# Seven products instead of eight: Strassen's scheme in the last MLP stage of an attention and MLP kernel

## The chip, the cores and the metric

The kernel runs on one core of a Trainium2 chip. The metric is the device time of one execution in microseconds (us). The engines are named as in the profile: PE (TensorE), DVE (VectorE), ACT (ScalarE), POOL (GpSimd) and SP (SyncE, which here only issues DMAs).

## The reference

```python
def attention(q, k, v, g_q, g_k):             # (8, 12, 448, 64) each, gains of 64
    q_n, k_n = rmsnorm(q, g_q), rmsnorm(k, g_k)
    scores = q_n @ k_n.T / 8
    attn = softmax(scores)                    # over the keys
    return attn @ v                           # f32

def mlp(x, w_in, w_out, alpha):               # x: 3584 x 768, w_in: 768 x 2048, w_out: 2048 x 768
    h = x @ w_in
    g = maximum(h, 0) + alpha * minimum(h, 0) # alpha: one slope for each of the 2048 columns
    return g @ w_out                          # f32

out = mlp(attention(...) as rows of tokens, w_in, w_out, alpha)
```

## The kernel before

The kernel works batch by batch (`B` = 8). The heads of a batch are taken in three groups of four heads (24 groups `y` in all). For each group q and k are loaded (tiles `nat`), squared on POOL (`sq`), summed on DVE, turned into a reciprocal root on ACT, and scaled (`qs`, line 179, on POOL for the later groups). A DMA on SP transposes them, and line 288 multiplies the transposed k by the gains on DVE. Then come the scores (`sc`), the exponentials (`expT`, ACT, line 343), the denominators and the products with v, whose result is `xT`.

For the third group of each later batch the denominator is prepared on POOL: `add_up` (line 356) adds the seven `expT` slices of the group into `rden` in six additions, and `den_pre` multiplies the sum by ones on PE (`dnb`, line 389). What follows `dnb` is a chain: two copies on DVE (line 397), a logarithm and an exponential on ACT (lines 401 and 410), a multiplication on DVE that writes `xT` (line 439).

The MLP runs one batch behind the attention. Its first product is cut into 16 units of 128 columns for each batch (`up`: six matmuls of 448 columns, ACT scales the result by alpha into `ah`, line 494, and DVE takes the maximum of both into `gT`, line 498). `gT` holds two batches side by side: 128 partitions by 16 column blocks (`NF`) by 896 tokens (`W`), the even batch in the first 448 tokens. Its second product is cut into units of one tile of 128 tokens and one half of the 768 outputs (`down`: 16 matmuls of 384 columns, a copy out of PSUM on DVE, line 520, and two stores of 64 rows, line 528). A pair of batches has 7 token tiles, and so 14 `down` units. The last unit of all is done in two halves of 192 columns with a store for each, half of its rows through ACT's queue.

The order on each engine is the order in which the Python code calls. A planner spreads the `up` and `down` units of a batch over the gaps between the attention steps of the next batch. Work that belongs to no gap is put behind a step with `after`. When the attention of the last batch is done, a list `rest` is left: the 16 `up` units of the last batch, one `down` unit left over from the even batch ahead of every third of them (`old`, five units: one of token tile 0, two each of tiles 1 and 2), and then the eight `down` units of tiles 3 to 6 (`new`):

```python
    ups, old, new = periods[B - 1]
    rest = []
    for n, u in enumerate(ups):
        if n % 3 == 0 and old:
            rest.append(old.pop(0)[1:])
        rest.append(u[1:])
    rest += [u[1:] for u in old + new]
```

PSUM has three pools: `pss` (tag `sc`, two tiles of two banks), `psa` (tag `acc`, one tile of two banks) and `psf` (tag `mm`, two banks). Units of `rest` take their bank from `psf`, every third from `psa`. In SBUF, `nat` has 6 buffers, `sq` 4, `qs` 4, `expT` `EB` = 3 and the result tiles `osb` 4.

Of the kernel before, what the change touches and what calls it, by code (L numbers as in the profile page):

```python
# [9 lines left out]
FP32 = mybir.dt.float32  # L10
FP16 = mybir.dt.float16
# [10 lines left out]
def kernel(  # L22
# [12 lines left out]
    nc = tc.nc  # L35

    B, H, S, D = q.shape
    DM = H * D
    DF = moe_w_in.shape[1]
    J = S // 64  # L40
# [3 lines left out]
    NF = DF // 128  # L44
    OH = DM // 2
# [4 lines left out]
    EB = 3  # L50
# [5 lines left out]
    ld = ctx.enter_context(tc.tile_pool(name="ld", bufs=2))  # L56
    att = ctx.enter_context(tc.tile_pool(name="att", bufs=2))
    ffn = ctx.enter_context(tc.tile_pool(name="ffn", bufs=2))
    pss = ctx.enter_context(tc.tile_pool(name="pss", bufs=2, space=bass.MemoryType.PSUM))
    psa = ctx.enter_context(tc.tile_pool(name="psa", bufs=1, space=bass.MemoryType.PSUM))  # L60
    psf = ctx.enter_context(tc.tile_pool(name="psf", bufs=2, space=bass.MemoryType.PSUM))
# [7 lines left out]
    out4 = out.rearrange("(b p j) m -> b j p m", b=B, j=J)  # L69
# [20 lines left out]
    w_out_sb = cst.tile([128, NF, DM], FP16, name="w_out_sb", tag="w_out_sb")  # L90
    gT = cst.tile([128, NF, W], FP16, name="gT", tag="gT")
# [4 lines left out]
    nat, sqs, qs, ss_t, rr_t, qkT, vt, xT = {}, {}, {}, {}, {}, {}, {}, {}  # L96
# [220 lines left out]
    expT, rden, scs = {}, {}, {}  # L317

    def pre(ys):
        return len(ys) == 1 and ys[0] >= PRE and ys[0] % G == G - 1  # L320
# [179 lines left out]
    def down(b0, t, oh, jobs=(), spare=False):  # L500
# [24 lines left out]
        for c in range(parts):  # L525
            for half in range(2):
# [3 lines left out]
                    in_=o[ds(64 * half, 64), ts(c, PW)],  # L530
                )

    def spin(count, wide=True):

        ps = psf.tile([128, 512], FP32, name="spin", tag="mm")
        for _ in range(count):
            nc.tensor.matmul(
                out=ps[:, :S], lhsT=idle32[:, :128] if wide else ident,
                rhs=idle32 if wide else idle, start=True, stop=True,
            )  # L540
# [5 lines left out]
    den_at, av_at, split = {}, {}, {}  # L546
# [4 lines left out]
    m = 0  # L551
    while m < NG * J or steps:
        n = len(bursts)
# [20 lines left out]
        while len(bursts[n]) < limit and m < NG * J:  # L574
            y, j = divmod(m, J)
# [11 lines left out]
    prep, post, roots, mid = {}, {}, {}, {}  # L587
# [4 lines left out]
    def after(n, f, *a):  # L592
        post.setdefault(max(int(n), 0), []).append((f, a))
# [11 lines left out]
    for y in range(G, NG):  # L605

        early = y < G + 2
        if early:
            n = turn_at[y - 1] + 1
        elif y == G + 2:  # L610
            n = den_at[G - 1]
        elif y == 2 * G:
            n = turn_at[y] - 4
        elif y % G == 1:
            n = den_at[y - 4] - 1 - pre((y - 2,))
        elif y % G:
            n = den_at[y - G] - pre((y - G,))
        else:
            n = av_at[y - 4]
# [22 lines left out]
    for b in range(B):  # L642
        ups = [(UP / 3 if b == 0 and ft < 4 else UP, up, (b, ft)) for ft in range(NF)]
        odd = b % 2
        new = [
            (DOWN, down, (b - odd, t, oh))
            for t in (range(3, J) if odd else range(3)) for oh in range(2)
        ]
# [16 lines left out]
    first = av_at[G - 1]  # L665
    gaps = [[] for _ in range(NB)]
    for b in range(B - 1):
        lo, hi = av_at[G * b + G - 1], av_at[G * b + 2 * G - 1]
        ups, old, new = (list(u) for u in periods[b])
        mlp = sum(u[0] for u in ups + old + new)  # L670
        stop = hi
# [5 lines left out]
        for n in range(lo, hi):  # L677
            clock += cost(n)
            free = True
            while ups or old or new:  # L680
                two = n in dens and pre(dens[n]) and len(gaps[n]) < 2
                if old and (not ups or (free or two) and (
                    wide(n) or len(old) > sum(wide(c) for c in range(n, hi))
                )):
                    u = old.pop(0)
                elif ups:
                    u = ups.pop(0)
                else:
                    u = new.pop(0)
# [12 lines left out]
                if n < hi - 1 and not short and clock + ahead > per * (n - lo + 1):  # L702
                    break
    ups, old, new = periods[B - 1]
    rest = []
    for n, u in enumerate(ups):
        if n % 3 == 0 and old:
            rest.append(old.pop(0)[1:])
        rest.append(u[1:])
    rest += [u[1:] for u in old + new]  # L710

    for n in range(1, NB):

# [7 lines left out]
    for n, g in enumerate((g_q, g_k)):  # L721
        for h in range(2):
            nc.gpsimd.dma_start(
                out=rows[NF + n : NF + n + 1, ds(64 * h, 64)], in_=g.unsqueeze(0)
            )
    load_qk(1, True)
    load_qk(2)

    spin(2)
    spin(17, False)  # L730
    ct = psf.tile([128, 512], FP32, name="ct", tag="mm")
    nc.tensor.transpose(ct[:, : NF + 2], rows, ident32[: NF + 2, : NF + 2])
    K0 = 3
    both, full, lo, hi = slice(0, 2), slice(0, J), slice(0, K0), slice(K0, J)
    for h in range(2):
        part_square("q", slice(h, h + 1), full, nc.scalar)
    for h in range(2):
# [13 lines left out]
        out=gain, in0=cols[:, NF : NF + 1], in1=cols[:, NF + 1 : NF + 2]  # L751
# [25 lines left out]
    for nm in "qk":  # L777
        after(first, square, 2 * G, nm)
    mid[4] = 2

    since = 2
    for n in range(NB):
# [6 lines left out]
        for t in first_tiles:  # L789
            if t == (0, J - 2):  # L790
                spin(1)
            elif t == (1, J - 3):
                spin(2, False)
            elif t == (1, J - 2):
                spin(1, False)
            elif t == (0, J - 1):
                turn_one(1, "q")
            elif t == (1, 0):
                turn_one(1, "k")
            elif t == (1, J - 1):  # L800
                turn(2)
            score(*t)
            if n == den_at[G - 1] - 1 and t == tiles[-1]:
                begin(0)
                begin(1)
            elif lead and t == tiles[0]:
                soft(*t)
                den(dens[n])
                attv(avs[n], 0, True, (log, invert))
            elif lead and t == tiles[1]:  # L810
                begin(2)
# [32 lines left out]
        if n in roots:  # L844
            y = roots[n]
# [41 lines left out]
        for k, (f, a) in enumerate(gaps[n]):  # L887
# [3 lines left out]
            else:  # L891
                f(*a, spare)
                done += 1
                if n in jobs and not (lead and done < 5) and (
                    n < av_at[2 * G - 1] or done % 2
                ):
                    g, c = jobs[n].pop(0)
# [3 lines left out]
                while late and done == late[0][0]:  # L901
                    _, g, c = late.pop(0)
# [11 lines left out]
                add_up(y, j)  # L914
        for f, a in jobs.pop(n, []) + post.get(n, []):
            f(*a)
    for k, (f, a) in enumerate(rest):
        f(*a, spare=k % 3 == 2)


# [28 lines left out]
```

## Time and profile before

| what | value |
|---|---|
| median of 3 runs | 427.22 us (427.17 to 427.23) |
| profiled execution, first to last instruction | 425.57 us (425.6 on the page) |
| between the two | 1.65 us |
| busy, share of the span: PE | 413.7 us, 97% |
| ACT | 275.3 us, 65% |
| POOL | 239.4 us, 56% |
| DVE | 222.4 us, 52% |
| granted TensorE clock, mean | 1.000 |

The profiled execution leaves no other time of its own than its span, so the span is set beside the median of the runs.

The page gives the busy time of each engine, the same in 40 slices, and the chain of work that ended last. In a row such as `372.40 1.14 PE hT L454 x6` the columns are the start in us from the start of the span, the time in us, and the instructions (engine, tile written, line, count). In rows of a timeline the bracket at the end is the idle time ahead of the instruction and what ended it. In rows of groups the figures behind the first bar are the busy time of all and the mean ns of one. Line numbers are those of the kernel before. Matmuls are pipelined, so a matmul's own duration is longer than the distance to the next one.

### The profile page before, as it was taken

What the parts mean: (1) busy time and instruction counts of PE and PEld (TensorE: products, weight loads), DVE (VectorE), ACT (ScalarE), POOL (GpSimd) and SP (SyncE); (2) the same over time, 40 slices, a digit from 0 to 9 for tenths busy, and PEclk for the clock granted to TensorE, in tenths of its full rate; (3) what the DMA queues carried; (4) which work ended last, traced back from release to release, by engine and by line L of the source; (5) the groups of instructions that cost most, each with busy time, mean ns of one, the idle gap of its engine ahead of it and who ended that gap; (6) DMA issues with size and microseconds to landing.
All of it is one profiled execution on the core that took longest, in us unless ns stands there. A gap on an engine that the chain in (4) does not pass through costs nothing.

```text
span 425.6 us, 11138 instructions
## 1 busy us (share of the span) xinstructions
PE 413.7 (97%) x4755; PEld 216.5 (51%) x4755; DVE 222.4 (52%) x331; ACT 275.3 (65%) x384; POOL 239.4 (56%) x173
## 2 busy tenths in 40 slices
PE   7889999999999999999999999999999999999996
PEld 3344454544455454544555545554555445555554
DVE  4875964456454636636564545647453343343421
ACT  5898887778856686578846677668847575332200
POOL 6789993494997299373984479482973009000000
PEclk9999999999999999999999999999999999999999
DMA  8999999999538965568455963545333500111033
GB/s 199 242 240 224 204 195 204 204 195 238 117 73 131 210 102 126 85 158 168 97 104 109 187 148 106 105 103 126 62 55 85 104 2 22 39 37 39 18 76 75
DMA packets 68529, 53.36 MB, mean 125 GB/s; under 512 B 35568, under 2 KB 68480, under 8 KB 68480
## 3 DMA queue, kind: packets, MB, share of 16 engines
q1 hardware_dynamic: 53680, 39.73, 42.5%
q0 software_dynamic: 13984, 11.81, 18.5%
q10 hardware_dynamic: 816, 1.11, 1.0%
q8 instruction: 37, 0.61, 0.6%
q14 instruction: 12, 0.10, 0.1%
HBM read 45.62 MB, written 11.01 MB: 133 GB/s over the span
## 4 chain that ended last, share of the span: by engine, by line
PE 86%; ACT 5%; DVE 4%; POOL 2%; issue 1%; ACTq 1%; POOLq 0%
PE op L508 29%; PE hT L454 21%; PE hTa L454 9%; PE sc L329 8%; PE opa L508 6%; PE av L368 5%; PE dn L368 3%; ACT expT L343 2%; PE avb L368 2%; PE dnb L389 2%; ACT ah L494 2%; DVE gT L498 1%; POOL sq L155 1%; DVE ss L163 1%; ACTq L108 1%
## 5 line engine op out<-in xcount | busy, mean ns | idle before, releaser
L343 ACT ACTIVATE expT<-sc,expb 128x896 f16<-128x896 f32 x168 | 161.3, 1003 | 42.8 <-PE sc L329 42.6
L508 PE MATMUL op<-w_out_sb,gT 128*128 128x384 f16 (+1 forms) x752 | 125.8, 323 | 0.5 <-DVE gT L498 0.5
L508 PEld LDWEIGHTS <-gT 128*128 128x128 f16 x912 | 86.0, 98 | 64.7 <-issue 11.8
L454 PE MATMUL hT<-xT,w_in_sb 128*128 128x448 f16 x552 | 114.7, 353 | 0.8 <-DVE gT L498 0.5
L179 POOL TENSOR_TENSOR qs<-nat,rr 128x896 f16<-128x896 f32 x41 | 68.4, 1690 | 82.4 <-issue 45.6
L454 PEld LDWEIGHTS <-w_in_sb 128*128 128x128 f16 x768 | 73.2, 98 | 73.8 <-issue 9.4
L494 ACT ACTIVATE ah<-hT,cols 128x448 f16<-128x448 f32 x91 | 57.4, 632 | 46.5 <-PE hT L454 45.6
L498 DVE TENSOR_TENSOR gT<-hT,ah 128x448 f16<-128x448 f32 x92 | 57.3, 623 | 50.7 <-ACT ah L494 49.8
L155 POOL TENSOR_TENSOR sq<-nat 128x896 f32<-128x896 f32 (+1 forms) x47 | 75.5, 1625 | 7.9 <-DMA nat<-in_q_dram 7.3
L520 DVE COPY osb<-op 128x384 f32<-128x384 f32 (+1 forms) x47 | 25.7, 548 | 69.3 <-PE op L508 68.9
L329 PE MATMUL sc<-qT,kT 64*32 64x448 f16 (+1 forms) x1092 | 54.0, 356 | 4.4 <-ACT expT L343 2.2
L356 POOL TENSOR_TENSOR rden<-rden,expT 128x896 f32<-128x896 f32 x30 | 56.8, 1895 | 2.4
L163 DVE TENSOR_REDUCE ss<-sq 128x14 f32<-128x896 f32 (+1 forms) x48 | 48.9, 1039 | 1.9 <-POOL sq L155 1.8
L454 PE MATMUL hTa<-xT,w_in_sb 128*128 128x448 f16 x204 | 44.1, 352 | 0.0
L494 ACT ACTIVATE ah<-hTa,cols 128x448 f16<-128x448 f32 x34 | 21.6, 634 | 21.0 <-PE hTa L454 20.9
L329 PEld LDWEIGHTS <-kT 64*32 64x32 f16 (+1 forms) x1092 | 17.0, 93 | 35.7 <-issue 29.3
L498 DVE TENSOR_TENSOR gT<-hTa,ah 128x448 f16<-128x448 f32 x34 | 21.2, 624 | 19.6 <-ACT ah L494 18.9
L439 DVE TENSOR_TENSOR xT<-av,rden 128x896 f16<-128x896 f32 x16 | 17.5, 1091 | 21.5 <-ACT rden L410 15.4
L368 PEld LDWEIGHTS <-vt 64*32 64x32 f16 (+1 forms) x1260 | 21.4, 94 | 12.7 <-issue 2.5
L508 PE MATMUL opa<-w_out_sb,gT 128*128 128x384 f16 x160 | 27.7, 326 | 0.0
L368 PE MATMUL av<-expT,vt 64*32 64x448 f16 (+1 forms) x812 | 26.6, 349 | 0.0
L356 POOL TENSOR_TENSOR rden<-expT 128x896 f32<-128x896 f16 x6 | 11.3, 1878 | 20.9 <-ACT expT L343 20.9
(67 smaller groups left out, 215.8 us busy)
## 6 DMA issues: line engine op xcount, KB each, us to landing
out_dram<-osb SPq DMA_DIRECT2D x109, 96.0 KB, 2.2
nat<-in_q_dram SPq DMA_DIRECT2D x46, 224.0 KB, 4.3
nat<-in_k_dram SPq DMA_DIRECT2D x46, 224.0 KB, 4.8
vt<-in_v_dram POOLq DMA_DIRECT2D x16, 336.0 KB, 5.9
w_in_sb<-in_moe_w_in_dram POOLq DMA_DIRECT2D x12, 256.0 KB, 7.2
w_out_sb<-in_moe_w_out_dram POOLq DMA_DIRECT2D x4, 768.0 KB, 11.1
nat<-in_q_dram ACTq DMA_DIRECT2D x2, 224.0 KB, 4.3
nat<-in_k_dram ACTq DMA_DIRECT2D x2, 224.0 KB, 5.7
```

The lines of the kernel that those rows point to most:

```text
L155: nc.gpsimd.tensor_mul(out=sqf[:, c], in0=src[:, c], in1=src[:, c])
L163: nc.vector.tensor_reduce(out=o[:, c], in_=sqs[y, nm][:, c], axis=AXIS_X, op=ALU.add)
L179: eng.tensor_mul(out=t.rearrange("p j h d -> p h j d"), in0=nat[y, nm], in1=rr_t[y][:, "qk".index(nm)].unsqueeze(3).broadcast_to((128, 2, ...
L329: nc.tensor.matmul(out=sc[ds(64 * g + m * c, m), par, :S].rearrange("p (j c) -> p j c", j=J), lhsT=kT[ds(64 * par, 64), j, g, ts(c, m)], r ...
L343: nc.scalar.activation(out=expT[y][:, j], in_=scs[y, j][:, :, :S], func=AF.Exp, scale=QK_SCALE, bias=expb[:, 0:1],)
L356: nc.gpsimd.tensor_add(out=s, in0=e[:, 0] if j == 1 else s, in1=e[:, j])
L368: nc.tensor.matmul(out=accs[g][ds(m * h, m), :S], lhsT=weights(g, y, par, ts(c, m), j), rhs=expT[y][ds(64 * g, 64), j, par, :], start=(j = ...
L454: nc.tensor.matmul(out=hT[:, :S], lhsT=w_in_sb[:, g * G + i, ts(ft, 128)], rhs=xT[b][:, g, i, :], start=(i == 0 and g == 0), stop=(i == G ...
L494: nc.scalar.activation(out=ah, in_=hT[:, :S], func=AF.Copy, scale=alpha_sb[:, ft : ft + 1])
L498: nc.vector.tensor_max(out=gT[:, ft, ds((b & 1) * S, S)], in0=hT[:, :S], in1=ah)
L508: nc.tensor.matmul(out=ops[c][:, :PW], lhsT=gT[:, ft, ts(t, 128)], rhs=w_out_sb[:, ft, ds(oh * OH + c * PW, PW)], start=(ft == 0), stop=(f ...
L520: nc.vector.tensor_copy(out=o[:, ts(c, PW)], in_=ops[c][:, :PW])
```

## The change

The `down` units of token tiles 1 to 6 of the last two batches are replaced. Two neighbouring token tiles, `t` and `t + 1`, and the two halves of the 2048 columns form a 2 x 2 grid of blocks of the left operand (A, `block`); the two halves of the 2048 rows and the two halves of the outputs form one of the right operand (`w_out`). Strassen's scheme, in Winograd's form, computes the 2 x 2 grid of results from seven block products instead of eight (`quad`, for t = 1, 3, 5). Each block product is eight matmuls of 384 columns.

The right operand's four differences (`tw`) are computed once by `mix_weights`: 16 subtractions of 128x768 f16 on POOL, in buffers of `nat` and `sq`, called behind the step that scales the last group. The left operand's four sums (`gs`) are computed by `mix` for each pair: four POOL operations of 128x1024 f16 in a buffer of `expT`. `mix(1)` is called ahead of `rest`, `mix(3)` and `mix(5)` behind it, and then the three `quad`s.

In `quad` the products go to four PSUM banks in the order x, y, p, z, x, z, p. Partial results are combined as they are read out of PSUM: `m1` and one result by copies on ACT, the others by additions on DVE. The pairs take their banks from `pss`, then `psa` and `psf`, then `pss` and `psf`. In the last pair the products into p are done in two halves of 192 columns, and half of the rows of the last result is stored through ACT's queue; all other stores go through SP. `rest` keeps the 16 `up` units and the one left-over `down` unit of tile 0.

```diff
+    def mix_weights():
+
+        def w(f, m, p):
+            return w_out_sb[:, ds(HF * f + QF * p, QF), ts(m, OH)]
+
+        for p in range(2):
+            for n in range(4):
+                tag, bufs = ("nat", 6) if (p, n) not in ((1, 2), (1, 3)) else ("sq", 4)
+                tw[n, p] = ld.tile([128, QF, OH], FP16, name="tw", tag=tag, bufs=bufs)
+        for n, x, y in (
+            (0, (0, 1), (0, 0)), (1, (1, 1), 0), (3, (1, 0), 1), (2, (1, 1), (0, 1))
+        ):
+            for p in range(2):
+                a = w(*x, p)
+                b = tw[y, p] if y in (0, 1) else w(*y, p)
+                for c in range(2):
+                    r = ts(c, QF // 2)
+                    nc.gpsimd.tensor_sub(out=tw[n, p][:, r], in0=a[:, r], in1=b[:, r])
+
+    def block(t, f):
+        return gT[:, ts(f, HF), ts(t, 128)]
+
+    def mix(t):
+
+        g = att.tile([128, 4, HF, 128], FP16, name="gs", tag="expT", bufs=EB)
+        mixes[t] = g
+        nc.gpsimd.tensor_add(out=g[:, 0], in0=block(t + 1, 0), in1=block(t + 1, 1))
+        nc.gpsimd.tensor_sub(out=g[:, 1], in0=g[:, 0], in1=block(t, 0))
+        nc.gpsimd.tensor_sub(out=g[:, 2], in0=block(t, 0), in1=block(t + 1, 0))
+        nc.gpsimd.tensor_sub(out=g[:, 3], in0=block(t, 1), in1=g[:, 1])
+
+    def send(b0, t, oh, o, c=slice(0, None), split=False):
+        for half in range(2):
+            bb, j = divmod(2 * t + half, J)
+            dst = out4[b0 + bb, j, :, ts(oh, OH)]
+            (nc.scalar if split and half else nc.sync).dma_start(
+                out=dst[:, c], in_=o[ds(64 * half, 64), c]
+            )
+
+    def quad(b0, t, wide, last=False):
...
+        product(x, block(t, 0), whole(0, 0), True)
+        m1 = part("m1")
+        nc.scalar.copy(out=m1, in_=x[:, :OH])
+        product(y, s2, mixed(1), True)
+        u2 = part("u2")
+        nc.vector.tensor_add(out=u2, in0=y[:, :OH], in1=m1)
+        for b, c in zip(ps, full):
+            product(b, s1, mixed(0), True, c)
+        product(z, s3, mixed(2), True)
+        u3 = part("u3")
+        nc.vector.tensor_add(out=u3, in0=z[:, :OH], in1=u2)
+        product(x, block(t, 1), whole(1, 0), False)
+        o = result()
+        nc.scalar.copy(out=o, in_=x[:, :OH])
+        send(b0, t, 0, o)
+        o = result()
+        for b, c in zip(ps, full):
+            nc.vector.tensor_add(out=o[:, c], in0=b[:, c], in1=u3[:, c])
+        send(b0, t + 1, 1, o)
+        product(z, block(t + 1, 1), mixed(3), False)
+        o = result()
+        nc.vector.tensor_add(out=o, in0=z[:, :OH], in1=u2)
+        send(b0, t + 1, 0, o)
+        o = result()
+        for b, c in zip(ps, full):
+            product(b, s4, whole(1, 1), False, c)
+            nc.vector.tensor_add(out=o[:, c], in0=b[:, c], in1=u2[:, c])
+            send(b0, t, 1, o, c, last)
...
     ups, old, new = periods[B - 1]
+    old = [u for u in old if u[2][1] == 0]
     rest = []
...
-    rest += [u[1:] for u in old + new]
...
     mid[4] = 2
+    after(max(roots), mix_weights)
...
+    mix(1)
     for k, (f, a) in enumerate(rest):
         f(*a, spare=k % 3 == 2)
+    mix(3)
+    mix(5)
+    for t in (1, 3, 5):
+        quad(B - 2, t, t != 3, t == 5)
```

More of the change, by code (lines that the diff above doesn't have):

```diff
@@ L531, in down @@
                 )
+    HF = NF // 2
+    QF = HF // 2
+    tw, mixes = {}, {}
+    def mix_weights():
[14 more added lines that the diff above has]
+                    nc.gpsimd.tensor_sub(out=tw[n, p][:, r], in0=a[:, r], in1=b[:, r])
@@ new lines, in quad, with whole, mixed, product @@
+    def quad(b0, t, wide, last=False):
+        s1, s2, s3, s4 = (mixes[t][:, n] for n in range(4))
+        if wide:
+            even, odd = (
+                pss.tile([128, 2, 512], FP32, name="oq", tag="sc") for _ in range(2)
+            )
+            x, p = even[:, 0], even[:, 1]
+        else:
+            odd = psa.tile([128, 2, 512], FP32, name="oqa", tag="acc")
+            x, p = (psf.tile([128, 512], FP32, name="oqm", tag="mm") for _ in range(2))
+        y, z = odd[:, 0], odd[:, 1]
+        full = (slice(0, OH),)
+        ps = [p]
+        if last:
+            full = (slice(0, OH // 2), slice(OH // 2, OH))
+            ps = [psf.tile([128, 512], FP32, name="oqm", tag="mm") for _ in range(2)]
+        def whole(f, m):
+            return lambda ft: w_out_sb[:, HF * f + ft, ts(m, OH)]
+        def mixed(n):
+            return lambda ft: tw[n, ft // QF][:, ft % QF]
+        def product(bank, g, v, first, c=slice(0, OH)):
+            for ft in range(HF):
+                nc.tensor.matmul(
+                    out=bank[:, c], lhsT=g[:, ft], rhs=v(ft)[:, c],
+                    start=(first and ft == 0), stop=(ft == HF - 1),
+                    skip_group_check=True,
+                )
+        def part(name):
+            return ld.tile([128, OH], FP32, name=name, tag="qs", bufs=4)
+        def result():
+            return ffn.tile([128, OH], FP32, name="osb", tag="osb", bufs=4)
+        product(x, block(t, 0), whole(0, 0), True)
[26 more added lines that the diff above has]
+            send(b0, t, 1, o, c, last)
```

## The prediction

> **What bounds the kernel now.** I read the page's forty slices first, then the chain that ended last over the final 100 us in order of time, then GpSimd's own timeline, and last the issuing queue of the stores.
>
> The slices, each about 10.6 us:
>
> ```profile
> PE   7889999999999999999999999999999999999996
> POOL 6789993494997299373984479482973009000000
> PEclk9999999999999999999999999999999999999999
> ```
>
> TensorE is full from the fourth slice to the last but one, at a granted clock that never moves, so time is won only by giving TensorE less to do and keeping it fed. GpSimd has two empty places near the end: two slices just ahead of its last 9, and the last six.
>
> The chain, around the last denominator and at the end (start us, us, what):
>
> ```profile
> 364.14 2.60 PE op L508 x16
> 366.74 1.06 PE dnb L389 x3
> ...
> 372.40 1.14 PE hT L454 x6
> ...
> 408.76 5.20 PE op L508 x32
> 413.96 2.60 PE opa L508 x16
> 416.56 5.25 PE op L508 x48
> 421.81 0.02 issue
> 421.84 0.36 DVE osb L520
> ```
>
> From 369.69 on it is TensorE alone: 13 units of the second product and 16 of the first, 13 x 2.60 + 16 x 1.14 = 52.0 us, which leads from 369.69 to 421.7. A 384-wide matmul is paced at 5.20 / 32 = 0.1625 us (the 323 ns of the cost groups count overlapping work), and the 32 of half width at the end at 2.65 / 32 = 0.083 us, so halving costs nothing.
>
> GpSimd's timeline from 326 us, and its costliest groups by form:
>
> ```profile
> 326.23 3.33 POOL L179 TENSOR_TENSOR qs<-nat,rr 128x896 f16<-128x896 f32 x2 [9.70 <-ACT rr L174]
> 350.48 1.88 POOL L356 TENSOR_TENSOR rden<-expT 128x896 f32<-128x896 f16 x1 [20.92 <-ACT expT L343]
> 352.43 9.79 POOL L356 TENSOR_TENSOR rden<-rden,expT 128x896 f32<-128x896 f32 x5
> L155 POOL TENSOR_TENSOR sq<-nat 128x896 f32<-128x896 f32 x43 | 71.9, 1690 | 7.9 <-DMA nat<-in_q_dram 7.3 <-DMA nat<-in_k_dram 0.4 <-DVE xT L439 0.2
> L155 POOL TENSOR_TENSOR sq<-nat 128x448 f32<-128x448 f32 x4 | 3.6, 925 | 0.0
> L356 POOL TENSOR_TENSOR rden<-expT 128x896 f32<-128x896 f16 x6 | 11.3, 1878 | 20.9 <-ACT expT L343 20.9
> ```
>
> Between the last scaling and the six sums of the last denominator it idles for 20.92 us. The sums end at 362.22; `dnb`, which reads them, starts at 366.74, straight behind a matmul group, so they are 4.5 us early.
>
> SyncE's queue, a pair of stores and the last store:
>
> ```profile
> 404.18 1.10 SPq L528 DMA_DIRECT2D out_dram<-osb  x2
> 422.22 0.47 SPq L528 DMA_DIRECT2D out_dram<-osb  x1
> ```
>
> A pair holds the queue for 1.1 us (the second starts 0.52 after the first and takes 0.59). Today a pair comes each 2.6 us.
>
> **Part 1, the products: -3.90 us.** Twelve units go (192 matmuls of full width, counting the halved unit as 16) and 3 x 7 x 8 = 168 come. 24 x 0.1625 = 3.90 us, all on the chain. There are 32 half-width matmuls before and after. The new operands have the old shapes, so I keep the old pace.
>
> **Part 2, the weight differences: +0.1 us, between 0 and 2.4.** Sixteen GpSimd subtractions of 128x768 f16 are queued right behind the last scaling, ahead of the six sums. They fill the 20.92 us idle place; beyond it they push the sums back, and TensorE waits at `dnb` once the sums' 4.5 us of slack is gone as well. With 0.1 for the semaphore, the cover is 20.9 + 4.4 = 25.3 us, or 1.58 us for each. Whatever exceeds it counts in full, for everything after `dnb` follows it: its copies, logarithm and exponential, xT, the first product of the last batch.
> No row subtracts f16 into f16. L155's two sizes give 925 ns at 448 and 1690 at 896, so 1.71 ns an element and 0.16 us fixed. On that line 768 elements take 1.47 us; two independent neighbours overlap by 0.05 (a pair of L179 takes 3.33 with 1.69 each), so 1.42 apart, 22.7 in all, hidden. The nearest row is `rden<-expT`, the one with two distinct f16 operands: 0.16 + (1.878 - 0.16) x 768 / 896 = 1.63, less 0.05 is 1.58 apart, 25.3 in all: just hidden. I take this one and charge 0.1. If each waits for the one before it as the five chained sums do ((9.79 - 1.89) / 4 = 1.975 apart, 0.09 more than their duration), it is 1.73 apart, 27.7 in all, and 2.4 us of stall. The order of instructions speaks for the lower value: neighbours write different tiles, and a difference that reads an earlier one stands four places behind it.
> The Trainium skill speaks against the place of these sums: "GPSIMD Engine Reference", section 3.1, gives a two-input tensor_tensor about 2.6 cycles an element, 4497 ns for 2048, and advises VectorE. By that page a subtraction would be an estimated 1.69 us, 27.0 in all, the stall 1.7 us and the kernel's time 426.6.
>
> **Part 3, a scaling on VectorE that meets them: +0.1 us.**
>
> ```profile
> L288 DVE TENSOR_SCALAR kT<-kT,gain x17: 443/707/1897, 82.6 to 338.6; 128x896 f16<-128x896 f16 x17
> ```
>
> It takes 0.44 us where GpSimd is idle and up to 1.90 where it is busy. The last one, at 338.64, now falls among the differences, so it grows by up to 1.45. Behind it on VectorE stands a `gT` that starts at 339.84; it would come up to 0.74 later and free its bank at 341.2, and the next user of that bank starts at 341.41. kT itself is read at 343.68. 0 to 0.2; I take 0.1.
>
> **Part 4, the token sums: 0.** Four GpSimd operations of 128x1024 a pair, at most 0.16 + 1.94 x 1.024 + 0.09 = 2.24 us each by the chained row. The first pair's are queued behind the six sums and read batch 6 alone (its last `gT` is at 365.5): done by 375, wanted at 391. The second and third pair's wait for the last unit of the first product. That ends 369.69 + 2.71 + 16 x 1.14 = 390.6 and is in `gT` 1.3 us later (0.63 ScalarE, 0.62 VectorE): 391.9. The first pair's seven products cover 7 x 1.30 = 9.1 us. S2 of the second pair is ready at 396.4 and wanted at 390.6 + 9.1 + 1.3 = 401.0; S2 of the third at 405.3, wanted at 410.1. Slack 4.6 us or more; it is gone at 3.0 us an operation (six from 391.9 to 410.1). Without the cover the eight would cost up to 18 us.
> The 16 first products now run without second products between them. Five in a row already run 1.14 apart (337.9 to 343.68 less a 0.5 us score); a bank is free 1.3 us after its product and comes up again 2.3 us after it: 0.
>
> **Part 5, reading the results out: 0.** Per pair VectorE does five additions and ScalarE two copies, about 0.6 us each by 0.56 for the 384-wide copy and 0.62 for the 448-wide two-input rows, in 9.1 us. The tightest wait: the fourth product's bank is read for 0.6 us and takes the sixth product 1.3 us after the fourth ended; margin 0.6. Without it each pair would lose some 0.6.
>
> **Part 6, the stores at the end: +1.5 us, between 0 and 2.1.** The last pair stores its four results in ten pieces, all behind its fifth product, eight of them through SyncE. Let E be the last matmul's end. The fifth product ends at E - 2.6, its ScalarE copy at E - 2.0; the queue, in its program's order, issues that pair from then to E - 0.9, the next (ready at E - 2.5) to E + 0.2, the third (its product ends at E - 1.3, added by E - 0.7) to E + 1.3, then the two half-width stores, the last starting at E + 1.9. Today the last starts at E + 0.41 (422.22 against 421.81). The end of the span, 3.35 us behind that issue, moves with it: +1.5. With the pace of the loads (1.25 a pair) and gaps it is 2.1; if the queue takes issues faster when it is full, down to 0.
>
> **Sum.** -3.90 + 0.1 + 0.1 + 0 + 0 + 1.5 = -2.2. The profiled span is 425.57, the median of the runs 427.22, so 1.65 us lies around the span, and I leave it: 425.57 - 2.2 + 1.65 = 425.0 us.
>
> **Rivals.**
> *The weight differences overflow their cover (0.20).* The spacing is 1.64 to 1.74 instead of 1.58; TensorE waits 1 to 2.5 us at `dnb`. For it: the six sums of this kernel are the slow GpSimd rows. Against: those are chained. Time 425.9 to 427.4.
> *The stores hide (0.15).* SyncE issues a full queue faster, or the half-width landings end no later. For it: a first issue of a pair shows 0.47 us, not 0.59. Time 423.3 to 424.2.
> *Slower (0.15): f16 into f16 is slower on GpSimd than any row here.* One mechanism, one place, the stall at `dnb`. It eats the whole remaining gain at 2.3 us of stall, 1.72 us apart, and is measurable as a loss from 1.78 us apart. At 2.0 us, 2.6 ns an element, the sixteen take 32.0, the stall is 6.7 and the time 431.6. Against it: the slowest spacing of the trace is 2.2 ns an element.
>
> **How the numbers follow.** The forecast with its stall below 1 us has 0.50, its own range 424.2 to 425.9. About 0.2% (0.85 us) is what a measurement can tell from no change, so faster means below 426.4. Faster: 0.50 + 0.15 + a quarter of the first rival = 0.70. Same: the rest of it, 0.15. Slower: 0.15. The range reaches from the hidden stores, 423.3, to the overflow's end, 427.4, and leaves out the slow case.
>
> **What would show it.** Right: 56 matmuls a pair in 9.1 us with no gaps; sixteen subtractions some 1.6 us apart from 329.5, the last sum ending near 366.5; `dnb` within 0.5 us of the matmuls before it; the last SyncE store starting 1.5 to 2 us behind the last matmul, and a span of 423.4. Wrong: `dnb` waiting for GpSimd by over 1 us; a product inside a pair waiting for VectorE; the last store within 0.6 us of the last matmul.

## The result and the profile after

The kernel after takes 425.32 us (425.23 to 426.15) against 427.23 for the kernel before on the same chip: a ratio of 0.9954, 95% interval 0.994 to 0.9968, 1.9 us faster. The prediction was 425.0. The span fell from 425.57 to 423.6 us, against a forecast of 423.4.

The runs of most kernels here, of the kernel before too, lie in two groups some 0.9 us apart; below, the lower groups are compared where that is said.

The slices of the kernel after:

```profile
PE   8789999999999999999999999999999999999994
POOL 6689994494996289382993569572982999940960
PEclk9999999999999999999999999999999999999998
```

GpSimd's two empty places are filled: the weight differences take the first, the token sums most of the second. TensorE is as full as before. The 8 at the end of the clock's line lies behind the last matmul, when TensorE has nothing left to do (in the stretch from 417.8 us on, the granted clock is 0.72, ahead of it 1.00).

The chain that ended last, from the sums of the last denominator (start us, us, what):

```profile
364.93 1.90 POOL rden L356
366.82 0.04 issue
366.87 1.00 PE dnb L389 x7
...
369.56 2.71 PE op L508 x16
372.27 1.13 PE hT L454 x6
...
390.43 9.12 PE oq L602 x56
...
416.47 1.33 PE oqm L602 x16
417.80 0.02 issue
417.83 0.36 DVE osb L640
```

Two things are to be seen. The last matmul ends at 417.80, where it was 421.81: 4.01 us earlier, 0.13 of which this execution was already ahead at 326 us (its last scaling starts at 326.10 instead of 326.23), so that 3.88 us is the change's. And GpSimd's six sums have come onto the chain: they end at 366.82, and `dnb`, for which TensorE has waited 0.26 us, starts 0.05 us behind. The differences fill their cover and pass it by 0.3 us.

GpSimd's timeline:

```profile
326.10 3.33 POOL L179 TENSOR_TENSOR qs<-nat,rr 128x896 f16<-128x896 f32 x2 [9.71 <-ACT rr L174]
329.40 6.43 POOL L554 TENSOR_TENSOR tw<-w_out_sb 128x768 f16<-128x768 f16 x4
335.78 12.97 POOL L554 TENSOR_TENSOR tw<-w_out_sb,tw 128x768 f16<-128x768 f16 x8
348.71 6.44 POOL L554 TENSOR_TENSOR tw<-w_out_sb 128x768 f16<-128x768 f16 x4
355.10 1.90 POOL L356 TENSOR_TENSOR rden<-expT 128x896 f32<-128x896 f16 x1
...
391.90 2.12 POOL L563 TENSOR_TENSOR gs<-gT 128x1024 f16<-128x1024 f16 x1 [16.64 <-DVE gT L498]
394.10 2.12 POOL L564 TENSOR_TENSOR gs<-gs,gT 128x1024 f16<-128x1024 f16 x1
```

Sixteen differences from 329.40 to 355.10 are 1.61 us apart.

The end, on SyncE's queue (the last pair's eight issues):

```profile
415.75 0.47 SPq L572 DMA_DIRECT2D out_dram<-osb  x1
416.27 0.60 SPq L572 DMA_DIRECT2D out_dram<-osb  x1
416.97 0.54 SPq L572 DMA_DIRECT2D out_dram<-osb  x1
417.87 0.47 SPq L572 DMA_DIRECT2D out_dram<-osb  x1
418.44 0.60 SPq L572 DMA_DIRECT2D out_dram<-osb  x1
419.10 0.58 SPq L572 DMA_DIRECT2D out_dram<-osb  x1
419.77 0.55 SPq L572 DMA_DIRECT2D out_dram<-osb  x1
420.42 0.56 SPq L572 DMA_DIRECT2D out_dram<-osb  x1
```

The last store is issued 2.62 us behind the last matmul, where it was 0.41. From the last matmul to the end of the span it is 5.8 us now and was 3.76. So the products gave 3.9 us and the stores took 2.0 of it back.

### The profile page after: what moved, and what is told of

Its sections match the earlier page's. It is cut to its first block, busy times and chain, and to the rows that moved or that the text cites. A ratio compares the mean times of both kernels' runs of the same rounds, so it can differ in the third digit from the quotient of the medians.

```text
span 423.6 us, 11137 instructions
## 1 busy us (share of the span) xinstructions
PE 410.0 (97%) x4731; PEld 214.3 (51%) x4731; DVE 224.4 (53%) x335; ACT 278.4 (66%) x390; POOL 290.1 (68%) x201
## 4 chain that ended last, share of the span: by engine, by line
PE 83%; ACT 6%; POOL 4%; DVE 4%; issue 1%; ACTq 1%; POOLq 0%
PE op L508 23%; PE hT L454 21%; PE hTa L454 8%; PE sc L329 8%; PE av L368 5%; PE opa L508 4%; PE oq L602 4%; PE dn L368 3%; ACT expT L343 3%; POOL rden L356 2%; PE avb L368 2%; PE oqm L602 2%; ACT ah L494 2%; PE dnb L389 2%; DVE gT L498 1%
## 5 line engine op out<-in xcount | busy, mean ns | idle before, releaser
L508 PE MATMUL op<-w_out_sb,gT 128*128 128x384 f16 x592 | 101.4, 326 | 0.5 <-DVE gT L498 0.5
L508 PEld LDWEIGHTS <-gT 128*128 128x128 f16 x704 | 66.1, 98 | 53.0 <-issue 11.8
L520 DVE COPY osb<-op 128x384 f32<-128x384 f32 x37 | 20.5, 555 | 54.4 <-PE op L508 54.0
L454 PE MATMUL hTa<-xT,w_in_sb 128*128 128x448 f16 x198 | 42.8, 352 | 0.0
L508 PE MATMUL opa<-w_out_sb,gT 128*128 128x384 f16 x112 | 19.4, 327 | 0.0
L563 POOL TENSOR_TENSOR gs<-gT 128x1024 f16<-128x1024 f16 x3 | 6.4, 2117 | 16.6 <-DVE gT L498 16.6
```

Of the source, the lines that this page charges most:

```text
L454: nc.tensor.matmul(out=hT[:, :S], lhsT=w_in_sb[:, g * G + i, ts(ft, 128)], rhs=xT[b][:, g, i, :], start=(i == 0 and g == 0), stop=(i == G ...
L508: nc.tensor.matmul(out=ops[c][:, :PW], lhsT=gT[:, ft, ts(t, 128)], rhs=w_out_sb[:, ft, ds(oh * OH + c * PW, PW)], start=(ft == 0), stop=(f ...
```

## The experiments

My theory after this: the gain is 24 matmuls at full pace; the stores in SyncE's queue take half of it back; the weight differences are hidden to within 0.1 us; and nothing else moves. The rivals are named with each run.

### 1. The last stores through two queues

```diff
-        send(b0, t, 0, o)
+        send(b0, t, 0, o, split=last)
...
-        send(b0, t + 1, 1, o)
+        send(b0, t + 1, 1, o, split=last)
...
-        send(b0, t + 1, 0, o)
+        send(b0, t + 1, 0, o, split=last)
```

> In the last pair all four results send half of their rows through ScalarE's queue, not only the last one. Theory (SyncE's queue, with eight issues in a row, sets the end): the last SyncE store starts 0.4 us behind the last matmul instead of 2.6 us, the end follows, and the time falls by about 2.1 us, from 425.3 to 423.2 us; the matmuls stay as they are. Rival (the bytes themselves, six tiles of 96 KB and two of 48 KB within some 3 us, set the end): the issues come earlier but land later, and the time falls by less than 0.8 us.

Measured: 423.78 us (423.62 to 423.86), a ratio of 0.9911 to the kernel before (0.9898 to 0.9924). It gained 1.5 us on the kernel after, not the 2.1 expected, and beats both kernels. The issues that now end last, from the timeline of the queues:

```profile
418.62 0.55 SPq L572 DMA_DIRECT2D out_dram<-osb  x1
418.89 0.56 ACTq L572 DMA_DIRECT2D out_dram<-osb  x1
```

and the last matmul's end, from the chain:

```profile
417.93 0.02 issue
```

The last issue on SyncE starts 0.7 us behind the last matmul and on ScalarE 1.0, not 0.4: three stores in a row still queue on each. The span ends 3.2 us behind ScalarE's last issue, as it ends 3.2 behind SyncE's in the kernel after. The rival, that the bytes bind, is out: the same bytes leave in less time and the end moves with the issues.

### 2. The first result early

In each pair the second product into x comes third, and x, y, x, z, p, z, p is the order of the banks:

```diff
         nc.vector.tensor_add(out=u2, in0=y[:, :OH], in1=m1)
-        for b, c in zip(ps, full):
-            product(b, s1, mixed(0), True, c)
-        product(z, s3, mixed(2), True)
-        u3 = part("u3")
-        nc.vector.tensor_add(out=u3, in0=z[:, :OH], in1=u2)
         product(x, block(t, 1), whole(1, 0), False)
         o = result()
         nc.scalar.copy(out=o, in_=x[:, :OH])
         send(b0, t, 0, o)
+        product(z, s3, mixed(2), True)
+        u3 = part("u3")
+        nc.vector.tensor_add(out=u3, in0=z[:, :OH], in1=u2)
+        for b, c in zip(ps, full):
+            product(b, s1, mixed(0), True, c)
...
```

> In each pair the product that completes the first result (second into x) comes third instead of fifth; the stores stay on SyncE. Theory (queue of SyncE): in the last pair the first two stores leave 2.6 us earlier and are out of the way of the others; the last SyncE store starts about 1.1 us behind the last matmul instead of 2.6, and the time falls by about 1.5 us to 423.8 us. Rival (the bytes or a fixed cost at the end): less than 0.5 us. If one of the moved products waited for VectorE or ScalarE, gaps of 0.3 to 0.6 us a pair would show on TensorE.

Measured: 425.51 us, but with runs from 424.44 to 426.49; the ratio, 0.9951 (0.9934 to 0.9967), does not part it from the kernel after. Its profile does. That execution had lost 0.7 us before the last batch (the second product ahead of it starts at 370.27 instead of 369.56), the pairs have no gaps, and the end is shorter. The end of the last matmul in the chain, and the last issue in SyncE's timeline:

```profile
418.49 0.02 issue
```

```profile
419.81 0.57 SPq L572 DMA_DIRECT2D out_dram<-osb  x1
```

The last issue is at 1.32 us behind the last matmul instead of 2.62, the end of the span at 4.4 instead of 5.8: the expected 1.4 to 1.5 us. In the lower groups of the times only 0.8 us of it is seen (424.44 against 425.23), half of what was expected. In the six runs of this kernel 2.08 to 2.15 us lie between span and time, in those of the kernel after 1.72 to 1.85; why is open.

### 3. Half of the weight differences later

```diff
-    after(max(roots), mix_weights)
+    after(max(roots), mix_weights, (0, 1))
...
+    mix_weights((2, 3))
     mix(1)
```

> Eight of the sixteen weight differences are made behind the six sums of the last denominator instead of ahead of them. Theory (the differences just fit their cover, and the 0.1 us by which the sums' end passes the old start of dnb is made good by the copies that dnb waits for anyway): dnb starts right behind the matmuls ahead of it, and the time stays at 425.3 us, within 0.2 us. Rival (the late sums cost a hidden part of the gain): the time falls by 0.3 us or more.

Measured: 425.61 us (425.56 to 426.49), a ratio of 0.9963 (0.9951 to 0.9975); the lower group is 0.3 us above that of the kernel after. The chain:

```profile
366.55 1.06 PE dnb L389 x3
...
369.50 2.71 PE op L508 x16
...
417.74 0.02 issue
```

`dnb` is back at its old place, 0.32 us earlier than in the kernel after, but the product behind it starts only 0.06 us earlier, and the last matmul ends only 0.06 us earlier. By these 0.06 us this execution was already ahead at GpSimd's last scaling (326.04 against 326.10).

Where the sums are in time, `dnb` and the products with v behind it take 2.95 us, because the second of `dnb`'s banks waits for the copy out of the product ahead (0.6 us by the profile's waits); where the sums are late, half of that wait is over meanwhile (0.3 us are left) and they take 2.69. Counted from the last scaling, the product behind `dnb` starts 43.46 us later in the kernel before, in the kernel after and here. So the late sums, 0.26 us late by this count, cost nothing, and on the chain the theory holds.

The time was not within the 0.2 us expected. The 0.3 us that this kernel is slower lie behind its last store: its profile has an 8 KB load of the instruction queue in the last microseconds, which that of the kernel after has not. The stores' issues are at the same places (the last at 420.36), so that load may be the 0.3; this is not shown, for it was not tried by itself.

### 4. No cover for the token sums

```diff
-    for t in (1, 3, 5):
-        quad(B - 2, t, t != 3, t == 5)
+    for t in (3, 1, 5):
+        quad(B - 2, t, t != 1, t == 5)
```

> The pairs are done in the order of tiles 3-4, 1-2, 5-6, so that nothing covers the token sums of tiles 3-4 (the pair that comes second now has the banks of the second one). Theory (the token sums are hidden by the first pair's products alone): the second product of the first pair waits for S2, which is ready at 396.2 where it would start at 391.7; a stall of 4.5 us and a time of 429.8 us. Rival (GpSimd's sums overlap more, or TensorE waits less): under 3 us.

Measured: 432.6 us (432.0 to 432.87), a ratio of 1.0117 (1.0104 to 1.013): 7.3 us over the kernel after, 2.8 more than expected. The timeline of TensorE (in the bracket its idle time and what ended it):

```profile
397.07 5.75 PE L602 MATMUL oq<-tw,gs 128*128 128x384 f16 x24 [4.53 <-POOL gs L564]
```

The same by stretches (the granted clock is the column behind the five engines' busy times):

```profile
390.00:397.00 7.00, 2.54 (x15) 1.21 (x13) 1.54 (x3) 1.74 (x3) 4.21 (x3) 1.00 0.00 0
397.00:398.00 1.00, 0.93 (x4) 0.51 (x5) 0.00 (x0) 0.00 (x0) 1.00 (x2) 0.68 0.00 0
398.00:399.00 1.00, 1.00 (x4) 0.45 (x3) 0.00 (x0) 0.00 (x0) 1.00 (x1) 0.50 0.08 16
399.00:400.00 1.00, 1.00 (x5) 0.46 (x4) 0.33 (x1) 0.00 (x0) 1.00 (x2) 0.50 0.00 0
400.00:401.00 1.00, 1.00 (x5) 0.55 (x4) 0.23 (x1) 0.00 (x0) 1.00 (x1) 0.61 0.00 0
401.00:402.00 1.00, 1.00 (x8) 0.59 (x6) 0.00 (x0) 0.00 (x0) 1.00 (x2) 1.00 0.00 0
```

The stall is 4.53 us, as worked out. Behind it the granted clock is 0.50 for 3.4 us and the matmuls are 0.32 us apart instead of 0.1625: 48 of them take 9.67 us instead of 7.80, another 1.9 us. The rest, 0.8 us, this execution had lost before (`dnb` starts at 367.65 instead of 366.87). The Trainium skill says of it, in "TensorE: Matmul & The Clock Gate", Part 1, that an idle window of about 3.4 us takes the array to half its clock; the trace agrees, with 4.53 us idle and 3.4 us at 0.50.

### 5 and 6. More weight differences

Two (experiment 5) or four (experiment 6, `n == 2` alone as the condition) of the sixteen are made twice, which changes no value. The edit of experiment 5:

```diff
-                    nc.gpsimd.tensor_sub(out=tw[n, p][:, r], in0=a[:, r], in1=b[:, r])
+                    for _ in range(2 if n == 2 and p == 1 else 1):
+                        nc.gpsimd.tensor_sub(out=tw[n, p][:, r], in0=a[:, r], in1=b[:, r])
```

> Two of the sixteen weight differences are made twice, so that GpSimd's eighteen take 3.2 us longer (1.61 us each). Theory (the cover of the differences is used up, and each further microsecond is TensorE's at dnb): dnb starts 3.2 us later and the time goes up by 3.2 us, from 425.3 to 428.5 us. Rival (there is cover left): under 2 us. Rival (the idle TensorE also loses its clock, as it did behind a stall of 4.5 us): 1.7 us more, 430.2 us; the idle time would be 3.5 us, near the 3.4 us for which the clock was halved.

> Four of the sixteen weight differences are made twice: 6.4 us more on GpSimd. Theory (each further microsecond counts in full, and a stall of over 4 us costs half the clock for 3.4 us behind it): dnb starts 6.4 us later, TensorE idles for 6.7 us and then runs for 3.4 us at half its clock, which costs up to 1.7 us more: 433.4 us in place of 425.3. Rival (no clock loss here, since the chain behind dnb is not TensorE's own): 431.7 us.

Measured: 432.06 us for two (runs of 432.04, 432.08 and 432.12, and one of 429.66), a ratio of 1.0083 (1.005 to 1.0116); 433.92 us for four (433.88 to 434.68), a ratio of 1.0149 (1.0134 to 1.0165). TensorE's wait at `dnb` in its timeline, with two more:

```profile
371.17 1.75 PE L389 MATMUL dnb<-rden,ones 64*32 64x448 f32 x16 [3.68 <-POOL rden L356]
```

GpSimd's timeline there (four differences and the two repeats; the kernel after has the four in 6.44 us):

```profile
349.58 9.89 POOL L555 TENSOR_TENSOR tw<-w_out_sb 128x768 f16<-128x768 f16 x6
```

The clock in and behind that wait, by stretches:

```profile
370.20:371.50 1.30, 0.33 (x8) 0.23 (x16) 0.00 (x0) 0.00 (x0) 1.30 (x2) 0.54 0.11 24
371.50:373.00 1.50, 1.50 (x24) 0.39 (x16) 0.00 (x0) 0.00 (x0) 1.50 (x1) 0.50 0.00 0
373.00:375.00 2.00, 2.00 (x56) 0.97 (x40) 1.16 (x2) 0.67 (x1) 1.92 (x2) 0.50 0.03 8
375.00:377.00 2.00, 2.00 (x21) 0.74 (x6) 0.71 (x1) 1.23 (x2) 2.00 (x2) 0.50 0.00 0
377.00:379.00 2.00, 2.00 (x13) 1.23 (x12) 0.38 (x1) 0.00 (x0) 2.00 (x2) 0.96 0.00 0
```

The wait with four more, in TensorE's timeline:

```profile
373.80 1.75 PE L389 MATMUL dnb<-rden,ones 64*32 64x448 f32 x16 [7.11 <-POOL rden L356]
```

and the stretches in which its clock falls and comes back (0.50 in all between them):

```profile
366.50:370.20 3.70, 0.18 (x2) 0.00 (x0) 0.56 (x1) 0.00 (x0) 3.54 (x3) 0.90 0.25 53
379.00:381.00 2.00, 2.00 (x12) 1.11 (x11) 1.00 (x1) 0.00 (x0) 2.00 (x2) 0.83 0.00 0
```

The wait grows by 7.11 - 3.68 = 3.43 us for two more differences, so there was no cover left. But a repeated difference costs more than the 1.61 us expected: it writes the tile that the operation ahead of it writes, and two repeats add 9.89 - 6.44 = 3.45 us, 1.73 each, the spacing that the prediction worked out for operations that wait for the one before.

And in both the clock is halved as well. With two more it is low from 370.3 to 377.1 us, of which 0.9 us still lie in the wait, through `dnb`, the products with v and most of a second product; with four more from 369.5 to 379.7. In the profiled execution with two more, the first product of the last batch starts at 379.05 instead of 372.27: 6.8 us, of which 0.9 came before 327 us and 3.4 to 3.5 are the two repeats. The clock cost 2.5: from `dnb` to that product it is 7.9 us, in the kernel after 5.4 (with four more 7.8). This is more than the 1.7 us of the rival, which had counted 3.4 us of low clock.

The run of 429.66 is 4.34 us above the kernel after, which is what the repeats and an early loss of 0.9 us make without any loss to the clock. Its mean granted clock on record, 0.992 against 0.986 in the other three, fits that; without a profile it stays an inference. So a stall of about 3.7 us stands at the edge. With four more, the profiled run is the slowest, at a mean clock of 0.986; the other three take 433.9 us at 0.989 and have no profile.

### 7. Eight products again

```diff
         product(x, block(t, 0), whole(0, 0), True)
+        product(x, block(t, 0), whole(0, 0), True)
```

> The first product of each pair is computed twice, so that a pair has eight products again. Theory (the whole gain comes from the 56 in place of 64 matmuls of a pair, at 0.1625 us each): 3.9 us more, 429.2 us; that is above the kernel before, by the 2.0 us that the stores cost at the end. Rival (part of the gain comes from the order or the banks): under 3.5 or over 4.3 us more.

Measured: 430.09 us (430.05 to 430.2), a ratio of 1.0056 (1.0041 to 1.0071): 4.8 us above the kernel after. The pairs:

```profile
391.31 10.42 PE oq L602 x64
...
421.25 1.33 PE oqm L602 x16
422.58 0.03 issue
```

From the first matmul of the pairs to the last it is 31.27 us here and 27.37 in the kernel after: 3.90 us, the number expected. The other 0.9 us this execution lost before 327 us (GpSimd's last scaling starts at 326.98 instead of 326.10), where its granted clock is 0.92 in the stretch from 13 to 26 us. All four runs lie within 0.15 us of each other; against the upper run of the kernel after (426.15) the difference is 3.9.

### 8. Both remedies for the end

The edits of experiments 1 and 2 together.

> Both remedies for the end together: the first result of a pair is complete after its third product, and in the last pair every result sends half of its rows through ScalarE's queue. Theory (a queue that issues three stores in a row takes some 0.64 us for each, and the last of them sets the end): each queue has at most two issues behind the last full-width result; the last store starts 0.5 us behind the last matmul (0.9 with the two queues alone, 0.4 in the kernel before), and the time falls from 423.7 to 423.3 us. Rival (what is left at the end is the landing): no change against 423.7 us.

Measured: 423.88 us (423.8 to 423.97), a ratio of 0.9911 (0.9896 to 0.9925), the same as with the two queues alone. Its span is 421.9 us against 422.1, and the last issues start 0.5 us (SyncE) and 0.8 us (ScalarE) behind the last matmul, 0.2 earlier than with the two queues alone; but the time did not follow, and the 423.3 expected was missed: 2.1 us lies between span and time here, as in experiment 2, and 1.7 with the two queues alone. Which of the two is better is not settled; either takes 3.4 us off the kernel before (lower groups).

## Why the prediction was right

*The products: -3.90 forecast.* Measured -3.88 at the last matmul, and 3.90 for the product put back in experiment 7. No wait inside a pair: 56 matmuls take 9.12 us. The sixteen first products in a row are 1.135 us apart (372.27 to 390.43), so they gained and lost nothing. (The stretch from 337.9 to 343.68 that the prediction read for them has no score in it: five products in 5.78 us, 1.16 apart.)

*The weight differences: +0.1 of 0 to 2.4.* They are 1.61 us apart (1.58 forecast), 25.7 us in all, and counted from the last scaling `dnb` starts 0.26 us late. The cost at the product behind it is nothing. The row of two distinct f16 operands was the right one to take: its duration scaled to 768 elements is 1.63 us, the measured one 1.64. The neighbours overlap by 0.03 instead of 0.05. "Whatever exceeds it counts in full" was not quite right: the first 0.26 us is won back, since `dnb`'s bank waits for a copy in any case, and what exceeds the cover by 3.4 us or more can cost the clock too. The rival with the overflow named 1 us of stall from 1.64 us apart. No run has that spacing; with the 0.26 already won back, 16 x 0.03 us more would be an estimated 0.5. The kernel stands that close to a loss.

The Trainium skill's figure ("GPSIMD Engine Reference", section 3.1), which is for f32, gave an estimated 1.69 us a subtraction; measured are 1.61 apart. That is a twentieth, but it is the difference between no stall and the 1.7 us that the prediction worked out for it: the place had no margin.

*The scaling on VectorE: +0.1.* VectorE's timeline of the kernel after, around its last scaling:

```profile
338.51 0.76 DVE L288 TENSOR_SCALAR kT<-kT,gain 128x896 f16<-128x896 f16 x1
339.72 0.62 DVE L498 TENSOR_TENSOR gT<-hT,ah 128x448 f16<-128x448 f32 x1 [0.44 <-ACT ah L494]
```

It met the differences and took 0.76 us instead of 0.44, but the `gT` behind it still waited 0.44 for ScalarE. It cost nothing.

*The token sums: 0.* 2.12 us each (at most 2.24 forecast). S2 of the second pair was ready at 396.2, wanted at 400.85. Experiment 4 shows what the cover is worth: 4.53 us of stall for one pair, as worked out, and 1.9 more for the clock, which the prediction's price without the cover had left out.

*Reading out: 0.* ScalarE's copies take 0.48 us and VectorE's additions 0.56, a little less than forecast.

*The stores: +1.5 of 0 to 2.1, measured +2.0.* This is the term that was mis-sized. The queue was right, and its order too; the pace was not. The forecast took 0.56 us an issue from a pair with a pause behind it. In a full queue the last five start 0.57 to 0.67 us apart, near the pace of the loads (1.25 us a pair) that the prediction kept for its upper end. And there is a gap of 0.36 us ahead of the fourth issue, at 417.87, though it stores the second half of a result whose first half the third issue stores. The kernel before has the same gap within a pair, where its queue was not full:

```profile
417.18 0.47 SPq L528 DMA_DIRECT2D out_dram<-osb  x1
418.01 0.47 SPq L528 DMA_DIRECT2D out_dram<-osb  x1
```

So such a gap needs no full queue; its cause is open. Seven issues took 4.67 us, where 3.9 was forecast, and the last started 2.62 us behind the last matmul, outside the 1.5 to 2 named as a sign of being right. The span ends 3.2 us behind that issue instead of 3.35, which gives a little back. The rival in which the stores hide is shown wrong by experiments 1 and 2, which take 1.4 to 1.6 us off the end of the span by issuing earlier alone.

*The sum.* -3.88 + 0 + 2.0 gives the -1.9 measured, against -2.2 forecast: what was charged too much for the differences and VectorE, 0.1 each, and too little for the stores, 0.5, partly cancelled. That the sum came within 0.3 us is in part luck.

## What to carry to other kernels

On a chain of one engine, work saved at that engine's measured spacing, not at its recorded durations, is what arrives at the end; then look at everything that the saving crowds together there, for a store queue that had 2.6 us for each pair of stores took half of this gain back when four results fell due within 3 us. Work moved into another engine's idle place must be priced to a few hundredths of a microsecond for each of its instructions when sixteen of them fill the place, and the row to take is the one with the same operand types. A stall of TensorE of 3.7 us or more is to be charged with the half clock behind it: that is what all three profiled runs with such a stall show, though one run without a profile seems to have escaped.

## What the runs showed of the hardware

I had not expected the clock. A wait of 4.53 us halved the granted clock for 3.4 us (1.9 us lost), and waits of 3.68 and 7.11 us halved it for 6.8 and 10.2 us, a part of which lies in the wait (2.5 us lost behind each). Worked out from the stretches shown, the clock was low from 397.4 to 400.8 us, from 370.3 to 377.1 and from 369.5 to 379.7. These lengths are once, twice and three times 3.4 us, and in each case the clock came back at the end of 3.4 us in which TensorE had no idle time. A part of the scatter of the runs has the same look: the profiled executions of experiments 2, 4, 5 and 7, which lost 0.7 to 0.9 us early, have a granted clock of 0.87 to 0.92 from 13 to 26 us; the other six profiles, of which none lost it, have 1.00 there.

GpSimd takes two f16 operands into f16 at 1.61 us for 768 elements and 2.08 us for 1024 (start to start, independent neighbours), which is 1.84 ns an element and 0.2 us fixed. Where a neighbour is not independent, it is 1.73 us for 768 elements (it writes the tile of the one before) and 2.20 for 1024 (it reads it).
